# One store of four rows, and the last matrix in pieces of 5, 6, 2 and 1: the tail of a decode block

## The chip, the cores and the metric

The kernel runs on one core of a Trainium2 chip. The metric is the device time of one execution in microseconds (us), the median of several runs; lower is better. A profile of one execution gives the details. PE is the engine of the matrix products, DVE the vector engine, ACT the engine of activations, POOL the fourth engine, SP the one that issues most transfers (DMAs).

## What is computed

One token goes through two layers in sequence, all tensors in bf16. With x of 512 elements:

```
h  = x + attention(layernorm(x))      # 32 query heads, 8 key heads, 16384 cached keys of 128
x1 = h + mix(gelu(layernorm(h) @ w1)) @ w2
out = h + x1 + gelu(layernorm(x1) @ w3) @ w4     # w3: 512 x 1792, w4: 1792 x 512
```

The sequence has length 1, and `mix` shifts each quarter of the row by one or two places along the sequence and pads with zeros. With one place nothing is left, so `mix(...)` is zero, x1 = h, and w1 and w2 are never read. So out = 2h + gelu(layernorm(h) @ w3) @ w4. Attention reads the key and value caches, and wq (512 x 4096) and wo (4096 x 512) as projections ahead of and behind it.

## The kernel before, in words

**Queues.** A class `Program` takes operations in the order of the source, finds from the tiles they read and write what each must wait for, and writes out one queue per engine (`emit`, line 95). An engine works through its queue in order. The `dve`, `act`, `pool` and `pe` helpers (lines 483 to 494) put an operation on its engine's queue; `load` (457) puts a transfer on SP's. A wait is an instruction's own or an instruction of its own at line 139.

**Branches.** Each of PE and DVE has one operation without a function (`dve(None)`, `pe(None)`). In its place the program writes a conditional branch that is never taken, with a hint that was marked at the engine's start (lines 146 to 156 for DVE, 221 and 336 for PE). DVE waits, ahead of its branch, for what that operation reads (line 151).

**Attention.** Four pairs of key heads are worked through in turn, with 4 MB of keys in halves and values per load. PE loops over the pairs. Behind them come the steps that this case is about:

- SP issues, at lines 738 to 746, the loads of wo (pieces of 16, 12 and 4 of 32 slices), w3 (2 and 2 of 4) and w4. w4 is cut along 14 blocks, `W4` at line 354, before in pieces of 4, 5, 4 and 1 blocks. A block is 128 KB; a partition gets 1 KB of each. All of them stand in one queue and are issued long before they land.
- The projection (L757): 32 slices of wo, four products at a time side by side in strips of 32 output rows. In front of slice 16, whose piece has not landed yet, `unread(6)` puts six products (L498) whose result nobody reads. They keep PE busy while it waits. A wait for the piece stands behind them.
- L762 copies the sum, L765 adds its parts, and `row_sums` (L508 to L524) adds x (the row `hr`, which is h), sums h and its squares, transposes it (`hT`), and leaves minus the mean and minus the mean square in `s[:, 0:2]`.
- ACT takes the mean off (L771, `hc`), PE multiplies by w3 (L777), then does four unread products.
- Meanwhile DVE computes one inverse root (`inverse_root` with n = 1, for the Gelu's scale `s[:, 7]`) and POOL another (n = 0, `s[:, 6]`, and L785 `s[:, 13]` = 1 + `s[:, 6]`). ACT helps at L552 with one product (`kw`) that DVE needs in its third round.
- ACT's Gelu runs in two halves (L788), and DVE transposes each (L792, `hcol`). The first transpose also waits for w4's first piece.
- The residual: ACT computes a bias from minus the mean and `s[:, 6]` (L797), then writes h times `s[:, 13]` plus that bias into the output's bank (L799), which needs the bank's earlier contents no more once the first transpose is done.
- The last products (L805) add the 14 blocks of w4 to it, four products of 128 columns each per block. A wait stands where a new piece begins. PE's branch stands in front of w4's second piece, DVE's (L795) behind the transposes, with a wait for w4's second piece.
- ACT copies the result out of the bank (`fin`, L810; the four quarters are in rows 0, 32, 64 and 96). Two stores (L814) of two rows each, one from SP and one from ACT, write it; SP waits for both (L816).

Of the kernel before, what the change touches and what calls it, by code (L numbers as in the profile page):

```python
# [10 lines left out]
ACTF = mybir.ActivationFunctionType  # L11
# [339 lines left out]
WO = ((0, 16), (16, 28), (28, 32))  # L351
VP = 2
W3 = ((0, 2), (2, 4))
W4 = ((0, 4), (4, 9), (9, 13), (13, 14))
PAIRS = HKV // 2
RPARTS = 6
QPAD = 4 * 7
# [10 lines left out]
def bass_sequential_preLN__gqa_block_cached__mixer_s_mlp__decode_kernel(  # L368
# [13 lines left out]
    with ExitStack() as ctx:  # L382
        sb = lambda name, shape, dt: ctx.enter_context(nc.sbuf_tensor(name, shape, dt))
        ps = lambda name, shape, dt: ctx.enter_context(nc.psum_tensor(name, shape, dt))
        P = Program(nc, ctx)
# [36 lines left out]
        bias = sb("bias", [128, 1], FP32)  # L422
# [9 lines left out]
        hr = sb("hr", [128, 128], FP32)  # L432
# [3 lines left out]
        xs = sb("xs", [128, 128], FP32)  # L436
        hg = sb("hg", [128, FQ], BF16)
        hT = sb("hT", [128, NCH, 32], FP32)
        hcol = sb("hcol", [128, NHC, 32], BF16)
        fin = sb("fin", [128, 128], BF16)  # L440
# [16 lines left out]
        def load(name, dst, src, key, by="SP", also=()):  # L457
            P.op(by, lambda e: e.dma_start(dst, src), w=[key, *also], dma=name)  # L458
# [24 lines left out]
        def dve(fn, r=(), w=(), bank=()):  # L483
            return P.op("DVE", fn, r, w, bank)

        def act(fn, r=(), w=(), bank=()):
            return P.op("ACT", fn, r, w, bank)
# [4 lines left out]
        def pe(fn, r=(), w=(), bank=(), also=()):  # L492

            return P.op("PE", fn, r, w, bank, also=also)

        def unread(times):
            field = qb[:, :, :, :].rearrange("p a j q -> p (a j q)")
            P.op("PE", lambda e: e.matmul(O_ps[1][:, :], field[:, 0:128], field[:, 0:512], start=True, stop=True),  # L498
                 r=["qb"], bank=[("O", 1)], times=times)

        def piece(cuts, m):
            return [lo <= m < hi for lo, hi in cuts].index(True)

        def copies(col, n):

            return col.to_broadcast([col.shape[0], n])
# [21 lines left out]
        def variances(i, ns):  # L528

            s, S = st[i], ("st", i)  # L530
            dve(lambda e: e.scalar_tensor_tensor(s[:, 2:3], s[:, 0:1], s[:, 0:1], s[:, 1:2],
                                                 ALU.mult, ALU.add), r=[(S, 0)], w=[(S, 2)])
            for n in ns:
                dve(lambda e, n=n: e.tensor_scalar(s[:, 4 + n:5 + n], s[:, 2:3], 0.0, -ADDED[n], ALU.min, ALU.add),  # L534
                    r=[(S, 2)], w=[(S, 4 + n)])

        def seeds(i, ns):

            s, t = st[i], sti[i]
            S, T = ("st", i), ("sti", i)  # L540
            lo, hi = min(ns), max(ns) + 1
            dve(lambda e: e.tensor_scalar(t[:, lo:hi], s[:, 4 + lo:4 + hi].bitcast(I32), -0.5, SEED,
                                          ALU.mult, ALU.add), r=[(S, 4 + n) for n in ns], w=[(T, n) for n in ns])

        def inverse_root(i, n, by, beside):
# [32 lines left out]
            r=["ident", "x4"], w=["quarter"])  # L578
# [11 lines left out]
            r=["ident_f"], w=["row32"])  # L590
        dve(lambda e: e.tensor_reduce(maskdd[:, :], ident_f[:, :].rearrange("p (n d) -> p d n", d=4), AX.X, ALU.add),
            r=["ident_f"], w=["maskdd"])
# [6 lines left out]
        for z, m, key, mk in ((zo, rowgh, "zo", "rowgh"), (zd, maskgh, "zd", "maskgh")):  # L599
# [5 lines left out]
            r=["hT", (("st", 0), 0), (("st", 0), 6)] + [("v", x) for x in range(VP)], w=["xn"])  # L605
# [3 lines left out]
        for i, key in enumerate(keys):  # L609
            P.part("query", i)  # L610
            for k in range(NCH):
                pe(lambda e, k=k: e.matmul(row[:, bass.ds(P.b + P.b0, 512)], copies(xn[:, k:k + 1], 128),  # L612
                                           wq_k[:, k, bass.ds(P.c + P.c0, REP * DH)], start=(k == 0), stop=(k == NCH - 1)),
                   r=["xn"], also=[("v", x) for x in range(VP)], w=["n" if key == "mn" else key], bank=[key])
        P.part()
        for g in range(2):
            half = banks[64 * g:64 * g + 64, PAIRS * g:PAIRS * g + PAIRS, :].rearrange("p j c -> p (j c)")
            for b in range(2):
# [3 lines left out]
                    r=["n" if x == "mn" else x for x in keys[PAIRS * g:PAIRS * g + PAIRS]], w=["qcol"],  # L622
                    bank=keys[PAIRS * g:PAIRS * g + PAIRS])
# [120 lines left out]
        w4_in = B_w4.rearrange("(p m) c -> p m c", p=128)  # L744
        for n, (lo, hi) in enumerate(W4):
            load(f"w4{n}", w4_sb[:, lo:hi, :], w4_in[:, lo:hi, :], ("r", 1, len(W3) + n))
# [3 lines left out]
            r=["o_m"], w=["o_f"])  # L750
        dve(lambda e: e.tensor_copy(o_b[:, :], o_f[:, :]), r=["o_f", ("r", 0, 0)], w=["o_b"])

        for r_ in range(32):
            q = r_ % 4
            if r_ == WO[1][0]:
                unread(6)
            pe(lambda e, r_=r_, q=q: e.matmul(O_ps[0][32 * q:32 * q + 32, :], copies(o_b[:, r_:r_ + 1], 32),  # L757
                                              wo_sb[:, r_ * D:(r_ + 1) * D], start=(r_ < 4), stop=(r_ >= 28)),
               r=["o_b"] + [("r", 0, n) for n in (piece(WO, r_),) if n], w=[("O", 0)], bank=[("O", 0)])
        h_ps, hkey = banks[:, 6, :], "spare0"  # L760
        for n in range(2):
            dve(lambda e, n=n: e.tensor_copy(osum[:, 256 * n:256 * n + 256], O_ps[0][:, 256 * n:256 * n + 256]),  # L762
                r=[("O", 0)], w=[("osum", n)], bank=[("O", 0)])
        for q in range(4):
            pe(lambda e, q=q: e.matmul(h_ps[32 * q:32 * q + 32, 0:128], copies(row32[:, 0:1], 32),  # L765
                                       osum[:, q * 128:(q + 1) * 128], start=True, stop=True),
               r=[("osum", q // 2), "row32"], w=[hkey], bank=[hkey])
        s = st[1]
        S = ("st", 1)
        row_sums(1, h_ps, hkey)  # L770
        act(lambda e: e.activation(hc[:, :, :], hT[:, :, :], ACTF.Identity, bias=s[:, 0:1], scale=1.0),  # L771
            r=["hT", (S, 0)] + [("r", 1, 0)], w=["hc"])


        for k in range(NCH):
            for q in range(4):
                pe(lambda e, k=k, q=q: e.matmul(s_ps[32 * q:32 * q + 32, 0, 0:FQ], hc[:, k, :],  # L777
                                                w3_sb[:, k, q * FQ:(q + 1) * FQ], start=(k == 0), stop=(k == NCH - 1)),
                   r=["hc"] + [("r", 1, n) for n in (piece(W3, k),) if n], w=[("s", 0)], bank=[("s", 0)])
        unread(4)  # L780
        variances(1, (0, 1))
        seeds(1, (0, 1))
        inverse_root(1, 1, dve, act)
# [2 lines left out]
        for n in range(2):  # L786
# [5 lines left out]
            dve(lambda e, lo=lo, hi=hi: e.transpose(  # L792
                hcol[:, lo:hi, :].rearrange("p m u -> p (m u)"),
                hg[:, :].rearrange("p (i m) -> p m i", m=NHC)[:, lo:hi, :]), r=[("hg", n)] + [("r", 1, len(W3))] * (n == 0), w=[("hcol", n)])
        dve(None, r=[("r", 1, len(W3) + 1)])  # L795

        act(lambda e: e.activation(s[:, 12:13], s[:, 0:1], ACTF.Identity, scale=s[:, 6:7]),  # L797
            r=[(S, 0), (S, 6)], w=[(S, 12)])
        act(lambda e: e.activation(h_ps[:, 0:128], hr[:, :], ACTF.Identity, bias=s[:, 12:13], scale=s[:, 13:14]),  # L799
            r=["hr", (S, 12), (S, 13), ("hcol", 0)], w=[hkey], bank=[hkey])  # L800
        for m in range(NHC):
            if m == W4[1][0]:
                pe(None)
            for o in range(4):
                pe(lambda e, m=m, o=o: e.matmul(  # L805
                    h_ps[32 * o:32 * o + 32, 0:128], hcol[:, m, :], w4_sb[:, m, o * 128:(o + 1) * 128],
                    start=False, stop=(m == NHC - 1), skip_group_check=True),
                   r=[("hcol", 1)] * (2 * m >= NHC) + [("r", 1, len(W3) + n) for n in (piece(W4, m),) if n],
                   w=[hkey], bank=[hkey], also=[("hcol", 0)] * (2 * m < NHC))
        act(lambda e: e.activation(fin[:, :], h_ps[:, 0:128], ACTF.Identity), r=[hkey], w=["fin"], bank=[hkey])  # L810

        rows = out[0, 0:1, :].rearrange("o (q j) -> (o q) j", q=4)
        for n, by in enumerate(("SP", "ACT")):
            P.op(by, lambda e, n=n: e.dma_start(rows[2 * n:2 * n + 2, :], fin[64 * n:64 * n + 64:32, :]),  # L814
                 r=["fin"], w=[("out", n)], dma=f"out{n}")
        P.op("SP", lambda e: e.nop(), r=[("out", 0), ("out", 1)])  # L816
        P.emit()

    return nc
# [28 lines left out]
```

## Time and profile before

| | us |
|---|---|
| median of 3 runs | 190.89 (190.88 to 191.0) |
| the profiled execution | 190.97 |
| its span, first to last instruction | 189.5 |
| mean granted PE clock | 0.887 |
| PE / DVE / ACT / POOL busy | 128.4 / 117.6 / 14.4 / 6.7 |
| read from memory | 79.17 MB, 418 GB/s over the span |

The page gives busy times by engine, the span in 40 slices, the DMA queues, the chain of work that ended last (followed back from the last instruction to what released it, step by step), and the costliest groups of instructions. In a group's line stand the source line (L805), the engine, the operation, what it writes and reads, shape and count, then busy time, mean duration of one, and the idle time before it with what ended it. The timeline has start, duration, engine, line and operation, and in brackets the idle time before. PEld are PE's weight loads; SPq, ACTq and the like are an engine's instruction queue. q1 and q10 are the DMA queues that SP and ACT feed, and queues marked "instruction" bring program code. The whole chain is, by line, to 45% loads of the keys, 14% loads of w3 and w4, 14% transposes of the keys and 9% products with them.

### The profile page before, as it was taken

To read this page: it belongs to the slowest core of one execution; us is meant where nothing else is said; L and a number is where in the kernel's file an instruction comes from. 1 tells how busy PE (TensorE), PEld (TensorE's weight loads), DVE (VectorE), ACT (ScalarE), POOL (GpSimd) and SP (SyncE) were. 2 spreads that over 40 slices of the span, in tenths; PEclk is the share of its full clock that TensorE was granted. 3 is DMA by queue.
4 is the path that set the end of the run, shared out by engine and by line. 5 is a ranking of instruction groups with operands and counts; after the bars stand their busy time and mean duration, and the time that the engine had idled before them with its cause. 6 is when DMAs were issued, how large, how long until landed. Compare 5 with 4: busy or idle time off the path is not lost.

```text
span 189.5 us, 2371 instructions
## 1 busy us (share of the span) xinstructions
PE 128.4 (68%) x743; PEld 48.0 (25%) x743; DVE 117.6 (62%) x151; ACT 14.4 (8%) x23; POOL 6.7 (4%) x15
## 2 busy tenths in 40 slices
PE   0109709996980498968703979696539996974874
PEld 0103203442230133322301423223113332231222
DVE  6740799995523989945038989460469896614270
ACT  3000200000400000004000000040000000500031
POOL 7100000000000000000000000000000000000040
PEclk9999985899999579996995899996978999998755
DMA  6999999999899999997999999999999989999992
GB/s 222 443 443 443 443 443 443 443 443 443 367 415 436 443 553 443 443 443 325 422 443 394 422 429 443 443 443 443 443 436 422 443 387 422 436 429 415 414 410 108
DMA packets 3330, 79.20 MB, mean 418 GB/s; under 512 B 384, under 2 KB 512, under 8 KB 1280
## 3 DMA queue, kind: packets, MB, share of 16 engines
q1 hardware_dynamic: 3316, 79.17, 97.5%
q8 instruction: 1, 0.02, 0.0%
q14 instruction: 1, 0.01, 0.0%
q10 hardware_dynamic: 12, 0.00, 0.0%
HBM read 79.17 MB, written 0.00 MB: 418 GB/s over the span
## 4 chain that ended last, share of the span: by engine, by line
DMA 66%; DVE 15%; PE 14%; issue 3%; SPq 1%; ACT 0%; DVEq 0%
DMA kb<-in_A_k_cache_dram 45%; DMA kb<-in_B_w_dram 14%; DVE kt L635 14%; PE banks L646 9%; DMA vb<-in_A_wq_dram 6%; PE banks L612 5%; SPq L458 1%; DVE qcol L619 1%; PE banks L805 0%; DVE qb L626 0%; DVE xn L603 0%; ACT fin L810 0%; SPq L139 0%; DVEq L139 0%; DVE qn L720 0%
## 5 line engine op out<-in xcount | busy, mean ns | idle before, releaser
L646 PE MATMUL banks<-kt,qn 128*128 x256 | 69.5, 415 | 25.3 <-DVE kt L635 23.9
L635 DVE STREAM_TRANSPOSE kt<-kb 128x2048 int32<-128x2048 int32 (+1 forms) x37 | 71.3, 1989 | 10.0 <-DMA kb<-in_A_k_cache_dram 8.4
L646 PEld LDWEIGHTS banks<-kt,qn 128*128 x256 | 26.3, 103 | 67.9 <-issue 51.8
L498 PE MATMUL banks<-qb 128*128 128x512 bf16 x58 | 22.3, 462 | 0.4
L686 PE MATMUL banks<-vb,pt 128*32 128x512 bf16 x256 | 16.4, 412 | 3.6 <-POOLq L473 2.9
L671 ACT ACTIVATE p_sb<-banks,bias 128x1024 bf16<-128x1024 f32 x4 | 4.5, 1114 | 132.6 <-DVE nmh L667 132.6
L702 DVE TENSOR_SCALAR od<-banks,rowc 128x128 f32<-128x128 f32 x4 | 1.4, 351 | 19.1 <-PE banks L686 19.1
L675 DVE STREAM_TRANSPOSE pt<-p_sb 64x1024 bf16<-64x1024 bf16 x8 | 9.9, 1239 | 5.4 <-ACT p_sb L671 5.3
L612 PE MATMUL banks<-vb,xn 128*128 x32 | 8.7, 440 | 6.1 <-DVE xn L603 6.1
L660 DVE TENSOR_REDUCE mx<-banks 128x1 f32<-128x1024 f32 x4 | 4.9, 1224 | 8.0 <-PE banks L646 8.0
L686 PEld LDWEIGHTS banks<-vb,pt 128*32 128x32 bf16 x256 | 7.0, 103 | 11.2 <-POOLq L473 3.1
L498 PEld LDWEIGHTS banks<-qb 128*128 128x128 bf16 x58 | 5.8, 104 | 15.4 <-issue 15.2
L619 DVE STREAM_TRANSPOSE qcol<-banks 64x1024 f32<-64x1024 f32 x4 | 4.8, 1227 | 6.9 <-PE banks L612 6.9
L554 POOL TENSOR_SCALAR st<-st 128x1 f32<-128x1 f32 x1 | 0.2, 246 | 175.9 <-DVE st L534 175.9
L663 PE MATMUL banks<-mxd,mean 128*128 128x128 f32 x8 | 2.0, 326 | 6.6 <-DVE mxd L661 6.6
L612 PEld LDWEIGHTS banks<-vb,xn 128*128 128x128 bf16 x32 | 3.5, 110 | 10.9 <-issue 8.3
L708 PE MATMUL banks<-od,zo 128*32 128x128 f32 x8 | 1.6, 285 | 6.5 <-DVE od L705 6.5
L655 ACT ACTIVATE banks<-mean 128x1024 f32<-128x1024 f32 x4 | 4.1, 1027 | 18.7 <-DVE qcol L619 18.6
L705 DVE SCALAR_TENSOR_TENSOR od<-banks,rowc,od 128x128 f32<-128x128 f32 x12 | 4.2, 350 | 0.4
L579 PE MATMUL banks<-x,quarter 4*128 4x128 bf16 x1 | 0.3, 284 | 6.0 <-DVE quarter L577 6.0
L576 DVE CAST ident<-ident_f 4x4 bf16<-4x4 f32 x1 | 3.8, 3848 | 0.6 <-POOL ident_f L571 0.6
L762 DVE COPY osum<-banks 128x256 f32<-128x256 f32 x2 | 0.8, 420 | 5.2 <-PE banks L757 5.2
(77 smaller groups left out, 45.6 us busy)
## 6 DMA issues: line engine op xcount, KB each, us to landing
kb<-in_A_k_cache_dram SPq DMA_DIRECT2D x8, 4096.0 KB, 29.7
vb<-in_A_v_cache_dram SPq DMA_DIRECT2D x2, 4096.0 KB, 29.5
vb<-in_A_wq_dram SPq DMA_DIRECT2D x1, 4096.0 KB, 12.2
kb<-in_A_wo_dram SPq DMA_DIRECT2D x1, 2048.0 KB, 25.0
kb<-in_B_w_dram SPq DMA_DIRECT2D x2, 896.0 KB, 23.2
kb<-in_A_wo_dram SPq DMA_DIRECT2D x1, 1536.0 KB, 28.3
kb<-in_B_w_dram SPq DMA_DIRECT2D x2, 512.0 KB, 25.9
kb<-in_B_w_dram SPq DMA_DIRECT2D x1, 640.0 KB, 26.0
```

The costliest lines, as they stand in the source:

```text
L498: P.op("PE", lambda e: e.matmul(O_ps[1][:, :], field[:, 0:128], field[:, 0:512], start=True, stop=True), r=["qb"], bank=[("O", 1)], times= ...
L576: dve(lambda e: e.tensor_copy(ident[:, :], ident_f[0:4, 0:4]), r=["ident_f"], w=["ident"])
L612: pe(lambda e, k=k: e.matmul(row[:, bass.ds(P.b + P.b0, 512)], copies(xn[:, k:k + 1], 128), wq_k[:, k, bass.ds(P.c + P.c0, REP * DH)], sta ...
L619: dve(lambda e, g=g, b=b, half=half: e.transpose(qcol[64 * g:64 * g + 64, 2 * b:2 * b + 2, :, :].rearrange("p e m u -> p (e m u)"), half.r ...
L635: P.op("DVE", lambda e, view=view: e.transpose(view(kt), view(kb[y])), r=[("r", y, i) for i in range(RPARTS)], w=[("kt", t + i) for i in r ...
L646: pe(lambda e, n=n: e.matmul(row[:, bass.ds(P.y, 512)], qn[:, n, bass.ds(P.q, 128)], key_piece(P.k, n), start=False, stop=(n == 3), skip_g ...
L655: act(lambda e: e.activation(s_all, copies(mean4[:, 0:1], 1024), ACTF.Identity, scale=0.0), r=["mean4", "p"], w=[("s", 0), ("s", 1)], **both)
L660: dve(lambda e: e.tensor_reduce(mx[:, :], s_all, AX.X, ALU.max), r=[("s", 0), ("s", 1)], w=["mx"], **both)
L671: act(lambda e: e.activation(p_sb[:, :], s_all, ACTF.Exp, bias=bias[:, 0:1], scale=float(SCALE), accum_out=acc[:, :]), r=[("s", 0), ("s", ...
L675: dve(lambda e, g=g: e.transpose(pt[64 * g:64 * g + 64, :, :, g, :], p_sb[64 * g:64 * g + 64, :]), r=["p"], w=["pt"])
L686: pe(lambda e, l=l, ct=ct, ch=ch: e.matmul(O_ps[0][32 * ct:32 * ct + 32, :], pt[:, l, ch, :, :].rearrange("p g u -> p (g u)"), tiles[:, l ...
L705: dve(lambda e, block=block, c=c: e.scalar_tensor_tensor(od[:, :], block, rowc[:, c:c + 1], od[:, :], ALU.mult, ALU.add), r=[key, "rowc", ...
```

## The change

Four edits, all in the tail:

1. `W4` becomes pieces of 5, 6, 2 and 1 blocks. PE's branch, which stands in front of the second piece, moves from block 4 to block 5.
2. The wait for the projection's second piece gets five unread products in place of six.
3. The residual's bias is minus `s[:, 0]`, known as soon as the mean is; `xs` holds h less its mean. Both are computed right behind L771 in source order, and L799 now forms (h - mean) times `s[:, 13]` plus the mean, which is the same value. The bias of L797 is gone. DVE's branch keeps its place in the source and waits for nothing.
4. One store of four rows from SP in place of the two.

```diff
-W4 = ((0, 4), (4, 9), (9, 13), (13, 14))
+W4 = ((0, 5), (5, 11), (11, 13), (13, 14))
...
             if r_ == WO[1][0]:
-                unread(6)
+                unread(5)
...
         unread(4)
+        act(lambda e: e.activation(s[:, 12:13], s[:, 0:1], ACTF.Identity, scale=-1.0), r=[(S, 0)], w=[(S, 12)])
+        act(lambda e: e.activation(xs[:, :], hr[:, :], ACTF.Identity, bias=s[:, 0:1], scale=1.0), r=["hr", (S, 0)], w=["xs"])
         variances(1, (0, 1))
...
-        dve(None, r=[("r", 1, len(W3) + 1)])
-
-        act(lambda e: e.activation(s[:, 12:13], s[:, 0:1], ACTF.Identity, scale=s[:, 6:7]),
-            r=[(S, 0), (S, 6)], w=[(S, 12)])
-        act(lambda e: e.activation(h_ps[:, 0:128], hr[:, :], ACTF.Identity, bias=s[:, 12:13], scale=s[:, 13:14]),
-            r=["hr", (S, 12), (S, 13), ("hcol", 0)], w=[hkey], bank=[hkey])
+        dve(None)
+
+        act(lambda e: e.activation(h_ps[:, 0:128], xs[:, :], ACTF.Identity, bias=s[:, 12:13], scale=s[:, 13:14]),
+            r=["xs", (S, 12), (S, 13), ("hcol", 0)], w=[hkey], bank=[hkey])
...
-        rows = out[0, 0:1, :].rearrange("o (q j) -> (o q) j", q=4)
-        for n, by in enumerate(("SP", "ACT")):
-            P.op(by, lambda e, n=n: e.dma_start(rows[2 * n:2 * n + 2, :], fin[64 * n:64 * n + 64:32, :]),
-                 r=["fin"], w=[("out", n)], dma=f"out{n}")
-        P.op("SP", lambda e: e.nop(), r=[("out", 0), ("out", 1)])
+        P.op("SP", lambda e: e.dma_start(out[0, 0:1, :].rearrange("o (q j) -> (o q) j", q=4), fin[0:128:32, :]),
+             r=["fin"], w=["out"], dma="out")
+        P.op("SP", lambda e: e.nop(), r=["out"])
```

## The prediction

> **What bounds the kernel now.** I read four views in this order: the chain of waits (which work ended last), the timeline of the last 17 us (who waits for whom), the stage windows (clock and DMA), the DMA view. Where merged lines hide single instructions, I read the same trace record by record, with its semaphore landings and DMA packets; times are from the span's start.
>
> The chain of waits ends so:
>
> ```profile
> 159.71 26.85 DMA kb<-in_B_w_dram
> ...
> 186.61 0.75 PE banks L805 x20
> 187.36 0.02 issue
> 187.38 0.28 ACT fin L810
> ```
>
> The end hangs on a weight load, not on arithmetic: the last 20 products of L805 wait for a piece of the last matrix. The timeline (start, duration, idle time and its releaser in brackets):
>
> ```profile
> 174.52 2.74 PE L498 MATMUL banks<-qb 128*128 128x512 bf16 x6
> ...
> 177.19 0.14 PEld L757 LDWEIGHTS banks<-kb,o_b 128*32 128x32 bf16 x8 [0.84 <-DMA kb<-in_A_wo_dram]
> ...
> 178.05 0.10 PEld L757 LDWEIGHTS banks<-kb,o_b 128*32 128x32 bf16 x4 [0.39 <-DMA kb<-in_A_wo_dram]
> ...
> 183.94 1.04 DVE L792 STREAM_TRANSPOSE hcol<-hg 128x224 bf16<-128x224 bf16 x2 [0.68 <-ACT hg L788]
> ...
> 184.24 0.30 ACT L797 ACTIVATE st<-st 128x1 f32<-128x1 f32 x1
> 184.29 0.23 POOL L785 TENSOR_SCALAR st<-st 128x1 f32<-128x1 f32 x1
> 184.63 0.46 ACT L799 ACTIVATE banks<-hr,st 128x128 f32<-128x128 f32 x1
> ...
> 185.15 1.15 PE L805 MATMUL banks<-kb,hcol 128*32 128x128 bf16 x36
> ...
> 186.61 0.72 PE L805 MATMUL banks<-kb,hcol 128*32 128x128 bf16 x20 [0.31 <-DMA kb<-in_B_w_dram]
> 187.38 0.28 ACT L810 ACTIVATE fin<-banks 128x128 bf16<-128x128 f32 x1 [2.29 <-PE banks L805]
> 187.68 0.60 SPq L814 DMA_DIRECT2D out_dram<-fin  x1
> 187.69 0.56 ACTq L814 DMA_DIRECT2D out_dram<-fin  x1
> ```
>
> The reader is to see the 36 + 20 split: blocks 0 to 8 run, then the engine waits for the piece with blocks 9 to 12. The landings (last of 16 increments) of the last matrix's pieces are 183.669, 185.253, 186.564 and 186.840; a product starts 0.042 after the landing it waits for (186.606). The stage windows (length, busy time and count of PE, PEld, DVE, ACT, POOL, then PE clock, DMA share, GB/s) show the clock:
>
> ```profile
> 174.10:177.50 3.40, 3.40 (x18) 0.87 (x14) 0.00 (x0) 0.00 (x0) 0.00 (x0) 0.50 0.99 408
> 177.50:180.90 3.40, 2.07 (x26) 0.79 (x18) 1.69 (x8) 0.00 (x0) 0.00 (x0) 1.00 0.99 411
> 180.90:184.30 3.40, 2.77 (x19) 0.71 (x20) 2.40 (x12) 1.48 (x5) 2.09 (x8) 0.50 1.02 414
> 184.30:187.70 3.40, 2.72 (x59) 1.34 (x56) 0.68 (x2) 0.97 (x3) 0.22 (x1) 0.50 0.54 206
> ```
>
> The DMA share is 0.99 or more until the weights are in, so bytes, not the cutting of them, set the last landing; and the tail runs at clock 0.50, one block (four products side by side) per 0.107 us.
>
> **The last matrix in pieces of 5, 6, 2, 1.** The bytes stay. Packets of 1, 4, 5 and 7 KB take 0.046, 0.161, 0.201 and 0.274 us each, eight per DMA engine and piece; between them I put 2 KB at 0.084 and 6 KB at 0.238. Old sum 8 x (0.161 + 0.201 + 0.161 + 0.046) = 4.55, new 8 x (0.201 + 0.238 + 0.084 + 0.046) = 4.55: the last landing stays at 186.84, I take 186.85. The others come at 182.384 (end of the matrix before) + 8 x 0.201 = 183.99; 185.253 + 2/4 of 1.311 = 185.91; about 186.57.
> Products before: first at 185.147, block 8 at 185.976, wait, block 9 at 186.606, blocks 10 to 13 at 186.689, 186.796, 186.903, 187.009; the last of these starts at 187.019, the copy out at 187.382. So block 13, landed at 186.84, starts 0.13 late because four blocks stand ahead of it behind one wait. After: blocks 0 to 4 from 185.17 to 185.7; wait for 185.91; blocks 5 to 10 start 185.95 to 186.46; block 11 at 186.61, 12 at 186.70; block 13 waits for its own landing, 186.89. Its fourth product starts 0.011 later and, as the ones right after a wait do, ends 0.288 later; the copy follows 0.049 after that: 187.24. **0.14 us less.** What is late next is the last landing itself. Blocks 0 to 4 and all that comes earlier now have cover: the first product may start as late as 186.89 - 13 x 0.107 + 0.025 = 185.52, against 185.17, so 0.35 us.
>
> **The residual's bias.** L797 (0.296) goes from behind both Gelus; a bias of 0.20 to 0.30 and a 128x128 pass of 0.40 to 0.46 (L771, L799) are put behind L771, which ends at 181.475. They end at about 182.2; queued behind them on ACT is L552 (0.202), which then ends at 182.45 instead of 181.78. DVE asks for it at 182.61: covered by 0.16, and the Gelu behind it waits for L777 anyway. L799 could then start when POOL's L785 is done (184.517) but also needs the first transpose. That one waits for piece 0, now at 183.99 instead of 183.669, and so starts at about 184.04 instead of 183.94, ends at 184.62: L799 at 184.66 instead of 184.634, first product at 185.17. The two edits cancel to +0.03, hidden by the 0.35.
>
> **Five unread products.** Six end so late that the projection resumes at 177.196, although its second piece landed at 176.725. Five end at about 176.77, 0.43 earlier. But the third piece lands at 178.004 and its products start at 178.049 either way: nothing. What is late next is that piece. PE stays busy through 174.1 to 177.5, so I expect no other clock behind it.
>
> **DVE's branch (L795) loses its wait** for piece 1. DVE's last transpose ends at 184.98 and nothing of it is left, so the wait itself cost nothing; the branch at 185.28 moves to about 184.5. Nothing is queued behind it but the program's end. What may follow it is a rival below. PE's branch moves one block on, 0.03.
>
> **One store.** The last copy ends 0.28 after it starts and both stores are issued within 0.03. SP's: issue 187.684, packets from 188.883, landed 189.239, so 1.555. ACT's: issue 187.689, packets from 189.154, landed 189.504, so 1.815; the span ends 0.023 later. SP's packets stand 0.010 apart. Nearest rows for four rows alone on a queue: SP's own two-row store (1.555) and the load of x4, four rows on ACT, 0.721 to 2.080, so 1.36, as one end; ACT's 1.815 as the other, if rows three and four cost what the second store did. Below nothing I exclude: two rows and four rows took ACT 0.565 and 0.564 to issue. I take SP's row, being the same queue and direction, plus 2 x 0.010: 1.575, so **0.24 us less**, with ends 0.00 and 0.46.
> The Trainium skill (DMA: Bandwidth & Descriptors, Why a DMA increments its semaphore by 16 and not by 1) says that such a DMA uses as many engines as its slowest dimension allows, from the lowest number on, and that the issuer writes the remaining increments at once: two stores of two rows then share two engines, one of four uses four. Here two landings follow an early one in each store, which agrees; the rows of the two stores do not overlap in time, so by that rule the sum is the same 0.24.
>
> **Sum.** The profiled execution took 190.97 (span 189.53 and 1.44 around it): 190.97 - 0.14 - 0.24 = 190.59. It stood 0.08 above the median 190.89, so the forecast is **190.50**. A measurement of this kernel can tell about 0.2%, or 0.38 us, from no change; the forecast lies on that line.
>
> **Rivals.**
> 1. *The early branch lets code loading into the weights' way; slower.* The only instruction packets of the span come after the two branches (185.236 on PE, 185.280 on DVE):
>
> ```profile
> q8 instruction: 1, 0.02, 2.2%
> q14 instruction: 1, 0.01, 0.7%
> ```
>
> One of 16 KB runs from 186.483 for 0.927, one of 8 KB from 187.120 for 0.307. The last weight packet ends at 186.38, on most engines at 186.08: now they miss each other by 0.1. If DVE's branch, 0.8 earlier, brings its packet 0.8 earlier, the 8 KB one falls at 186.3, the 16 KB one at 185.7. It decides from 186.38 on the slowest engine. Price: the last landing moves by up to 0.307 (190.50 + 0.31 = 190.81, within 0.2%) or 0.927 (190.50 + 0.93 = **191.43**, slower). For it: that timing. Against: one of 16 engines carries it, and others have 0.3 to spare. [...] 0.09 for the cheap, 0.07 for the dear one.
> 2. *The second pair of rows costs what the second store cost.* Store gain 0: 190.97 - 0.14 - 0.08 = 190.75. For: ACT's packets came 0.27 after SP's. Against: x4's four packets start within 0.072. 0.12.
> 3. *The lone store is as quick as x4's load.* Gain 0.46: 190.28. For: two issues ran side by side now. Against: SP's row. 0.14.
> 4. *The clock or ACT eats the cover.* If 177.5 to 180.9 ran at 0.50, L757's last products (0.389), L765 (0.74 busy) and L522 (0.38) lose some 0.5 together, 0.15 over the cover: 190.65. Against: PE is busy throughout the window before. 0.05.
> 5. *The weights' gain does not come*, the landings being as late as block 13 now starts: 190.64. 0.05.
>
> The forecast has 0.48. **Range 190.22 to 190.90**: rival 3 at its lower end, the cheap case of 1 at its upper, each with the 0.06 to 0.09 by which runs of this kernel stand apart; rivals 2, 4 and 5 lie inside, the dear case is left out. Faster by over 0.2%: rival 3 (0.14) and 0.35 of the forecast's 0.48 (a store without a second one beside it is more likely under than over SP's row): 0.49. Slower: the dear case and a little of the cheap one, 0.08. Within: the rest, 0.43.
>
> **What would show it.** Right: L805 in groups of 20, 24, 8, 4 with the last wait about 0.08, the copy out at 187.24, one store of about 1.58 to landing, L757's third piece still at 178.05. Wrong: a last weight landing past 187.0 beside an earlier instruction packet; a store with packets over 1.3 after issue; the first product after 185.52.

## The result, and the profile after

The changed kernel takes 191.61 us (median of 22 executions) against 190.85 for the kernel before in the same session: a ratio of 1.0034, 95% interval 1.0024 to 1.0043. It is slower by 0.76; 190.50 was forecast, with a range of 190.22 to 190.90. The executions of the changed kernel fall into two groups: 19 took 191.39 to 191.99, three took 190.49 to 190.65. The 22 of before all lie between 190.55 and 191.09. So the forecast time occurs, in one execution of seven, and something happens in the others. It happens within the span, the time from the first to the last instruction: the spans are 190.1 to 190.7 in the 19 and 189.2 to 189.3 in the three, and what an execution takes beyond its span is 1.27 to 1.45 in both groups.

The profiled execution took 191.87 and is one of the 19. Its chain of waits ends as forecast, on a small last group of products:

```profile
160.41 26.69 DMA kb<-in_B_w_dram
...
187.15 0.27 PE banks L805 x4
187.41 0.02 issue
187.44 0.28 ACT fin L810
```

The timeline of the tail (start, duration, idle time before and its releaser):

```profile
178.25 0.10 PEld L757 LDWEIGHTS banks<-kb,o_b 128*32 128x32 bf16 x4 [0.93 <-DMA kb<-in_A_wo_dram]
...
185.76 1.63 PE L805 MATMUL banks<-kb,hcol 128*32 128x128 bf16 x56
186.78 0.12 PEld L805 LDWEIGHTS banks<-kb,hcol 128*32 128x32 bf16 x8 [0.32 <-DMA kb<-in_B_w_dram]
187.14 0.10 PEld L805 LDWEIGHTS banks<-kb,hcol 128*32 128x32 bf16 x4 [0.24 <-DMA kb<-in_B_w_dram]
187.44 0.28 ACT L810 ACTIVATE fin<-banks 128x128 bf16<-128x128 f32 x1 [1.73 <-PE banks L805]
187.74 0.63 SPq L811 DMA_DIRECT2D out_dram<-fin  x1
```

The reader is to see that the products do what the pieces were cut for: 8 and then 4 wait for their own landings. The copy out starts at 187.44, against 187.38 before, because the last weights land 0.26 later in this execution (187.102 against 186.840; the third piece of the projection was already 0.20 later). From the last landing to the copy it takes 0.335, against 0.542; that this is the clock's doing and not the pieces' is shown further down.

Nothing up to the copy explains 0.9 us. The waits of SP's queue do. Their line for the store, before (engine, line, what it waited for, us in total, times, longest):

```profile
SPq L816 <- DMA out_dram<-fin: 1.2, 1, 1.2
```

and after:

```profile
SPq L813 <- DMA out_dram<-fin: 2.2, 1, 2.2
```

The store takes 2.79 from issue to its last landing (187.740 to 190.526); 1.575 was forecast. The DMA queues from 188.6 to 189.6 (packets, MB, share of the 16 engines), before:

```profile
q10 hardware_dynamic: 4, 0.00, 0.4%
q1 hardware_dynamic: 4, 0.00, 0.3%
```

and after:

```profile
q14 instruction: 1, 0.01, 3.5%
q1 hardware_dynamic: 8, 0.00, 0.7%
```

A packet of program code, 8 KB, now runs amid the store. Packet by packet: the rows leave at 188.968, 188.979 and 188.995; the code packet runs from 188.975 to 189.535; the fourth row leaves at 189.531. The first three rows have landed by 189.335, the fourth at 190.526. Before, the same kind of packet stood at 189.842, behind both stores' rows.

The account of the two executions: copy out 0.055 later; from the start of the copy to the last landing 3.089 against 2.122, 0.967 more; the rest of the execution's time, outside the stretch from the first instruction to the last landing, 1.34 against 1.47, 0.12 less. Together 0.90, which is 191.87 - 190.97.

### The profile page after: what moved, and what is told of

It is laid out like the page before. It is cut to its first block, busy times and chain, and to the rows that moved or that the text cites. A ratio compares the mean times of both kernels' runs of the same rounds, so it can differ in the third digit from the quotient of the medians.

```text
span 190.6 us, 2362 instructions
## 1 busy us (share of the span) xinstructions
PE 126.4 (66%) x737; PEld 47.5 (25%) x742; DVE 117.6 (62%) x151; ACT 14.4 (8%) x24; POOL 6.7 (3%) x15
## 4 chain that ended last, share of the span: by engine, by line
DMA 65%; DVE 17%; PE 10%; issue 5%; SPq 1%; ACT 0%; DVEq 0%
DMA kb<-in_A_k_cache_dram 45%; DVE kt L635 16%; DMA kb<-in_B_w_dram 14%; DMA vb<-in_A_wq_dram 7%; PE banks L612 5%; PE banks L646 5%; SPq L458 1%; DVE qcol L619 1%; DVE qb L626 0%; DVE xn L603 0%; ACT fin L810 0%; PE banks L805 0%; SPq L139 0%; DVEq L139 0%; DVE qn L720 0%
## 5 line engine op out<-in xcount | busy, mean ns | idle before, releaser
L646 PE MATMUL banks<-kt,qn 128*128 x256 | 70.4, 418 | 24.1 <-DVE kt L635 22.6
L498 PE MATMUL banks<-qb 128*128 128x512 bf16 x52 | 19.2, 406 | 0.5
L612 PE MATMUL banks<-vb,xn 128*128 x32 | 9.4, 464 | 6.4 <-DVE xn L603 6.4
L757 PE MATMUL banks<-kb,o_b 128*32 128x512 bf16 x32 | 2.3, 383 | 4.0 <-DMA kb<-in_A_wo_dram 2.8
```

The lines of the kernel that those rows point to most:

```text
L646: pe(lambda e, n=n: e.matmul(row[:, bass.ds(P.y, 512)], qn[:, n, bass.ds(P.q, 128)], key_piece(P.k, n), start=False, stop=(n == 3), skip_g ...
```

## The experiments

In the table, "DVE through" is when DVE's queue had passed its last instruction: the end of its branch, and in e6, whose branch stands far ahead, the start of its last transpose. (A free branch can end while a transpose still runs: in the changed kernel the last one ends at 185.56.) "Code 1, 2" are the starts of the two packets of q14, "rows" the leaving of the store's rows, "landed" the last row's landing, all from the profiled execution; "us" is the median of all executions, "over 191.3" how many of them. The kernel before took 190.74 to 190.85 in the four sessions.

| kernel | DVE through | code 1 | code 2 | rows | landed | us | over 191.3 |
|---|---|---|---|---|---|---|---|
| before | 185.35 | 187.12 | 189.84 | 188.88 to 189.16 | 189.50 | 190.85 | 0 of 22 |
| changed | 184.96 | 186.44 | 188.98 | 188.97 to 189.53 | 190.53 | 191.61 | 19 of 22 |
| e1 two stores | 184.74 | 186.36 | 188.96 | 188.97 to 189.25 | 189.64 | 190.87 | 0 of 11 |
| e2 store alone | 185.51 | 187.00 | 189.80 | 188.87 to 188.93 | 189.28 | 190.65 | 0 of 11 |
| e3 DVE's wait back | 186.05 | 187.53 | 189.97 | 188.80 to 188.86 | 189.21 | 190.89 | 0 of 11 |
| e4 ACT holds | 184.80 | 186.29 | 189.00 | 189.10 to 189.51 | 190.41 | 191.56 | 6 of 8 |
| e5 store, branch freed | 184.47 | 186.19 | 188.80 | 188.93 to 189.28 | 190.14 | 191.48 | 8 of 12 |
| e6 branch early | 184.66 | 186.24 | 188.84 | 188.85 to 189.25 | 190.19 | 191.54 | 5 of 5 |
| e7 branch on residual | 185.26 | 186.75 | 189.18 | 188.66 to 188.72 | 189.07 | 190.49 | 0 of 11 |
| e8 pieces, store, branch | 185.26 | 186.76 | 189.35 | 188.74 to 188.79 | 189.14 | 190.59 | 1 of 12 |
| e9 three and one | 184.63 | 186.13 | 189.04 | 188.51 to 189.23 | 189.63 | 190.92 | 0 of 11 |
| e10 DVE holds for the copy | 187.52 | 189.10 | 191.54 | 188.67 to 188.72 | 189.07 | 192.53 | 4 of 4 |
| e11 old pieces | 185.97 | 187.75 | 190.20 | 188.63 to 188.68 | 189.09 | 190.53 | 0 of 11 |

### Is it the store, and who moved the packet?

**e1**, the changed kernel with two stores again:

```diff
-        P.op("SP", lambda e: e.dma_start(out[0, 0:1, :].rearrange("o (q j) -> (o q) j", q=4), fin[0:128:32, :]),
+        for n, by in enumerate(("SP", "ACT")):
+            P.op(by, lambda e, n=n: e.dma_start(rows[2 * n:2 * n + 2, :], fin[64 * n:64 * n + 64:32, :]),
...
```

> The changed kernel with its store edit undone: two stores of two rows, one from SP and one from ACT. Theory A (a packet of program code stands ahead of the fourth row on its DMA engine; two rows go to two other engines): 190.75 us, 0.1 below the kernel before, no time over 191.2, and an instruction packet near 189.0 that harms nothing. Theory B (the loss is in the code packet itself, or in the new pieces, the residual or the branch): still 191.3 to 191.8.

190.87 (before, same session: 190.74; ratio 0.9996 to 1.0013). The queues of e1 from 188.6 to 189.6:

```profile
q14 instruction: 1, 0.01, 2.1%
q1 hardware_dynamic: 4, 0.00, 0.4%
q10 hardware_dynamic: 4, 0.00, 0.3%
```

The code packet is there, 188.964 to 189.306, and all four rows pass it: SP's leave at 188.965 and 188.980, ACT's at 189.241 and 189.248. So the loss needs the store of four rows, theory A.

**e2**, the kernel before with the one store alone:

```diff
-        for n, by in enumerate(("SP", "ACT")):
-            P.op(by, lambda e, n=n: e.dma_start(rows[2 * n:2 * n + 2, :], fin[64 * n:64 * n + 64:32, :]),
+        P.op("SP", lambda e: e.dma_start(out[0, 0:1, :].rearrange("o (q j) -> (o q) j", q=4), fin[0:128:32, :]),
...
```

> The kernel before with the one store of four rows alone. The third instruction packet stood at 189.84 before and at 188.98 after; two things could have moved it. Theory A1 (ACT, which issues no store any more, runs into its closing code sooner): the packet is near 189.0 here too, the fourth row waits, 191.4 us. Theory A2 (DVE's branch, freed of its wait, moves both of DVE's packets): the packet stays near 189.8, behind the rows, and the kernel takes 190.6.

190.65, against 190.74 for the kernel before in its session, ratio 0.9986 to 1.0004. The same window of e2:

```profile
q1 hardware_dynamic: 8, 0.00, 0.7%
```

Four rows and four increments, and no code; the packet stands at 189.803. The store alone is not the loss either, and ACT's earlier end does not move the packet: theory A2.

**e3**, the changed kernel with DVE's wait put back:

```diff
-        dve(None)
+        dve(None, r=[("r", 1, len(W3) + 1)])
```

> The changed kernel with the wait of DVE's branch for the last matrix's second piece put back; that piece now lands at about 186.0. Theory A2: the branch moves from 184.9 to 186.0, the third instruction packet behind the store's rows, 190.5 us with no time over 191. Theory A1: the third packet stays near 189.0, 191.5 us.

190.89. No execution is over 191.23 and the packet is at 189.966, as A2 has it. But the time is 0.4 above what I expected, and it lies beyond the span: all eleven executions take 1.55 to 1.95 more than their span of 189.0 to 189.4, against 1.27 to 1.49 for the kernel before. e10 returns to that.

**e4**, the changed kernel with ACT held until the store has landed:

```diff
         P.op("SP", lambda e: e.nop(), r=["out"])
+        P.op("ACT", lambda e: e.nop(), r=["out"])
```

> The changed kernel with one operation more: ACT waits for the store to land before it ends. Theory A1: no instruction packet before the landing, 190.5 us with no time over 191. Theory A2: no change, 191.5 us.

191.56, packet at 189.002, fourth row at 189.512, 3 ns before that packet ends. Theory A1 falls here too.

### Do the two edits suffice, and is it the branch?

**e5**, the kernel before with the one store and the freed branch, nothing else:

```diff
-        dve(None, r=[("r", 1, len(W3) + 1)])
+        dve(None)
...
-            P.op(by, lambda e, n=n: e.dma_start(rows[2 * n:2 * n + 2, :], fin[64 * n:64 * n + 64:32, :]),
...
+        P.op("SP", lambda e: e.dma_start(out[0, 0:1, :].rearrange("o (q j) -> (o q) j", q=4), fin[0:128:32, :]),
...
```

> The kernel before with two of the changed lines: one store of four rows, and DVE's branch without its wait; old pieces, old residual, six unread products. If these two together are the whole loss: branch at about 184.6, third instruction packet near 189.0, most times at 191.4 to 191.8. If the new pieces or the residual belong to it: 190.65 as with the store alone.

191.48, eight of twelve executions at 191.3 to 192, four at 190.6 to 190.8. Store and freed branch together make the loss; pieces, residual and unread products are not needed for it.

**e6**, the changed kernel with DVE's branch 11 us earlier:

```diff
         dve(lambda e: e.tensor_copy(o_b[:, :], o_f[:, :]), r=["o_f", ("r", 0, 0)], w=["o_b"])
+        dve(None)
...
-        dve(None)
```

> The changed kernel with DVE's branch 11 us earlier, behind the cast at L751 (about 173.3). If the third packet follows the first at a fixed distance of 2.4 to 2.8 us, both lie amid the weights at about 175 and 177.5, none near the store: 190.5 to 190.9, the weights' last landing up to 0.3 later. If the third packet is fetched when DVE is done with its code and not at a distance from the branch: it stays near 189 and the time at 191.5.

191.54. The branch ran at 173.248; no code packet followed for 13 us. The window of e6 from 188.6 to 189.6 is like that of the changed kernel:

```profile
q14 instruction: 1, 0.01, 2.6%
q1 hardware_dynamic: 8, 0.00, 0.7%
```

My theory that the packets follow the branch falls. They follow DVE's coming to the end of its queue: in every kernel of the table the first starts 1.5 to 1.8 us after DVE is through, the second 2.4 to 2.9 us behind the first. The wait mattered because it held DVE back, not because a branch stood behind it.

### Holding DVE to a chosen time

**e7**, the changed kernel with DVE held until the residual is in the bank:

```diff
-        dve(None)
...
         act(lambda e: e.activation(h_ps[:, 0:128], xs[:, :], ACTF.Identity, bias=s[:, 12:13], scale=s[:, 13:14]),
-            r=["xs", (S, 12), (S, 13), ("hcol", 0)], w=[hkey], bank=[hkey])
+            r=["xs", (S, 12), (S, 13), ("hcol", 0)], w=[hkey, "res"], bank=[hkey])
+        dve(None, r=["res"])
```

> The changed kernel with DVE's branch behind a wait for the residual (L799, done at about 185.2), as late as it stood before the change. Third packet near 189.8, behind the rows of the store; first packet behind the last weights: 190.5, 0.25 under the kernel before. If the branch's time is not what places the packet: 191.5.

190.49, ratio 0.9981 to 0.9999: the one kernel of this study that is under the one before beyond its interval, if barely. SP's wait for the store in e7:

```profile
SPq L813 <- DMA out_dram<-fin: 1.0, 1, 1.0
```

The reader is to compare it with the 2.2 of the changed kernel. The timeline of e7 shows all four groups of products that the forecast named:

```profile
185.21 0.46 PE L805 MATMUL banks<-kb,hcol 128*32 128x128 bf16 x20
...
185.84 0.52 PE L805 MATMUL banks<-kb,hcol 128*32 128x128 bf16 x24 [0.17 <-DMA kb<-in_B_w_dram]
186.54 0.12 PEld L805 LDWEIGHTS banks<-kb,hcol 128*32 128x32 bf16 x8 [0.37 <-DMA kb<-in_B_w_dram]
...
186.84 0.10 PEld L805 LDWEIGHTS banks<-kb,hcol 128*32 128x32 bf16 x4 [0.17 <-DMA kb<-in_B_w_dram]
187.13 0.28 ACT L810 ACTIVATE fin<-banks 128x128 bf16<-128x128 f32 x1 [1.98 <-PE banks L805]
187.43 0.63 SPq L811 DMA_DIRECT2D out_dram<-fin  x1
```

**e8**, e7 with the old residual and six unread products, that is, the kernel before with the new pieces, the one store and the held branch:

```diff
-W4 = ((0, 4), (4, 9), (9, 13), (13, 14))
+W4 = ((0, 5), (5, 11), (11, 13), (13, 14))
...
-        dve(None, r=[("r", 1, len(W3) + 1)])
...
             r=["hr", (S, 12), (S, 13), ("hcol", 0)], w=[hkey, "res"], bank=[hkey])
+        dve(None, r=["res"])
...
-            P.op(by, lambda e, n=n: e.dma_start(rows[2 * n:2 * n + 2, :], fin[64 * n:64 * n + 64:32, :]),
...
+        P.op("SP", lambda e: e.dma_start(out[0, 0:1, :].rearrange("o (q j) -> (o q) j", q=4), fin[0:128:32, :]),
...
```

> The kernel before with the new pieces, one store and DVE's branch behind a wait for the old residual (done at about 185.1); old residual, six unread products. Against the run before this one it lacks the residual and the fifth-for-sixth product, which I held to cost and gain nothing: 190.5 as there. Against the store alone (190.65) it adds the pieces: 0.14 less if the tail runs at the half clock, nothing if at the full one.

190.59, ratio 0.9991 to 1.001. Against e7 that is 0.10, less than the intervals tell apart: residual and unread product bring little or nothing. One execution of twelve took 191.52. It has no profile, but its times say that it is not like the 19 of the changed kernel: its span is 189.6, and it takes 1.92 beyond it. The executions over 191.3 of the changed kernel, e4, e5 and e6 have spans of 190.0 to 190.9 and take 1.27 to 1.51 beyond. In this it is like e3, to which e10 returns.

**e9**, the changed kernel (DVE free) with three rows from SP and the fourth from ACT:

```diff
-        P.op("SP", lambda e: e.dma_start(out[0, 0:1, :].rearrange("o (q j) -> (o q) j", q=4), fin[0:128:32, :]),
...
+        for n, (by, lo, hi) in enumerate((("SP", 0, 3), ("ACT", 3, 4))):
+            P.op(by, lambda e, lo=lo, hi=hi: e.dma_start(rows[lo:hi, :], fin[32 * lo:32 * hi:32, :]),
...
```

> The changed kernel (DVE free) with its store cut in two: rows one to three from SP, row four from ACT. Theory (the code packet occupies one DMA engine, the one that a store's fourth row goes to; the first three rows of every slow store left at once): no row meets it, 190.8 us as with two and two rows, nothing over 191.3, although the third instruction packet stands near 189.0. Rival (the code packet holds up whichever row is last in order, or any store near it): row four waits again, 191.5 us.

190.92, none over 191.17. The code packet runs from 189.043 to 189.350, and SP's three rows leave amid it, at 189.205, 189.221 and 189.232, and land by 189.63. So it is not any row near a code packet that waits, but a store's fourth; the others take other ways. (These rows left 1.42 after their issue, where a lone store's first row leaves after 1.2; the later of two stores does so in the kernel before as well, 1.47.)

**e10**, the changed kernel with DVE held until the last copy:

```diff
-        dve(None)
...
         act(lambda e: e.activation(fin[:, :], h_ps[:, 0:128], ACTF.Identity), r=[hkey], w=["fin"], bank=[hkey])
+        dve(None, r=["fin"])
```

> The changed kernel with DVE held in front of its branch until the last copy (L810, done at about 187.6), 2.4 us later than with the residual. Theory (DVE's closing code is fetched when DVE gets there, and the program ends only when that is done): first packet of DVE's at about 189.1, the second at about 191.7, the store untouched or hit by the first, and the time 1.5 to 2.5 us longer than 190.5: 192 to 193. Rival (only the meeting with the store matters): 190.5.

192.53, all four executions within 0.31. The store is as quick as in e7 (landed 189.067), the span as short (189.1 us), and still the execution is 2 us longer: it takes 3.3 us beyond its span. Both packets of q14 moved with DVE, by 2.35 and 2.36 against e7, the one of q8 did not (186.455 against 186.431). So these two packets of q14 are DVE's closing code, as I call it from here on (what they hold the trace does not tell), and the execution ends later when they come later. This fits e3: its span is 189.2, but its second packet ends at 190.33, and the execution takes 1.56 beyond the span against 1.31 in e7.

**e11**, e7 with the old pieces:

```diff
-W4 = ((0, 5), (5, 11), (11, 13), (13, 14))
+W4 = ((0, 4), (4, 9), (9, 13), (13, 14))
```

> The kernel of the run before with DVE's branch behind the residual, with the old pieces of 4, 5, 4 and 1 blocks. The difference to it (190.49) is what the new pieces bring: 0.14 if the tail is at the half clock in most executions, so 190.63; nothing if it is at the full one in most.

190.53, ratio 0.9982 to 1.0: the new pieces bring 0.04, nothing that these runs can tell. In its profile the last blocks are 0.056 apart, so at the full clock, and landing to copy takes 0.335 with the old pieces too. The profiled execution, at 191.03, is one of two of the eleven that took 1.93 beyond their span: DVE was through at 185.97, 0.7 later than in e7, and its second packet ran from 190.196 to 190.651, far behind the span's end at 189.127. One execution of e7 (191.03, 1.83 beyond its span) looks the same. So the held branch has a price too, in a few executions.

## Why the prediction was wrong, point by point

**The step that failed** is the one on DVE's branch: "Nothing is queued behind it but the program's end. What may follow it is a rival below." The program's end is code, and it comes by the same DMA engines as the store. Rival 1 followed that fetch only as far as the weights. It looked at the two instruction packets of the span, between 186.4 and 187.4; a third starts at 189.842, 0.3 behind the span's end, and I did not look there. It stood 0.95 behind the last of SP's rows. The edit moved it forward by 0.87, just as another edit gave the store a fourth row.

**The store** was the term mis-sized by it: 1.575 forecast, 2.79 measured in the changed kernel, 1.62 to 1.64 where no code is in the way (e2, e3, e7). So the rows I priced it from were right for one store, and their condition, an empty DMA engine, was not examined. The gain was too large as well. In e2's profile the landing is 0.23 earlier than before (189.276 against 189.504), as forecast, yet its median is only 0.09 lower and not distinguishable from none. It is not DVE's closing code that keeps the rest: beyond its span e2 takes 1.31 in the median, the kernel before 1.33. The spans themselves lie only 0.1 apart (medians 189.3 and 189.4, given to 0.1). So the two profiled executions differ by more than the two kernels do; why stays open.

**The forecast number came out by luck where it came out.** e7 takes 190.49 and three executions of the changed kernel 190.49 to 190.65, close to the 190.50 of the sum. But e7 is 0.25 under the kernel before of its session (190.74), where the sum had 0.38 from the pieces and the store; of these, the pieces bring nothing that can be told (e11) and the store alone about 0.1 (e2). What set the three executions apart from the 19 is not known either, as none of the three was profiled.

**Rivals.** Rival 1 had the right cause and the wrong place. The branch itself, to which it gave a part, has none: it is never taken, and in e6 it moved by 11 us without moving a packet. The first packet came where rival 1 put it, at 186.1 to 186.4 wherever DVE was free. Its cheap case may be seen in e1: the packet runs from 186.358 to 186.712, right behind the last weight packet (to 186.355), and one of the 16 landings comes at 187.133 where the other fifteen are in by 186.775; in the piece before the gap was 0.04. That would be the 0.3 of the cheap case. In the changed kernel, where the packet runs from 186.443 to 186.875 and the weights to 186.615, no landing stands apart like that. Its dear case did not occur: the 16 KB packet of q8 stayed at 186.3 or later in every kernel. Rival 2 is refuted by e2 (rows 0.059 apart), rival 3 as well (1.62, not 1.36). The forecast's 0.48 was too much for a sum that moved an engine's end without asking what follows it. All three signs of being wrong that the prediction named stand in the changed kernel's profile: a last landing past 187.0 (187.102) beside an earlier code packet, a row 1.79 after its issue, a first product at 185.76. Only the second cost what was lost.

**The pieces** gave the mechanism as forecast (groups of 20, 24, 8 and 4 in e7), but not the gain. I took the tail's clock of 0.50 as given. The half-speed stretches lie elsewhere in each execution: from 180.92 to the end in the trace of before, from 179.05 to 185.87 in that of the changed kernel. Its stage windows read:

```profile
174.10:177.50 3.40, 1.02 (x24) 0.65 (x21) 0.00 (x0) 0.00 (x0) 0.00 (x0) 1.00 0.98 407
177.50:180.90 3.40, 1.70 (x21) 0.49 (x13) 1.42 (x7) 0.00 (x0) 0.00 (x0) 0.73 1.00 414
180.90:184.30 3.40, 2.71 (x20) 1.14 (x21) 2.31 (x12) 1.19 (x5) 1.65 (x6) 0.50 1.02 420
184.30:187.70 3.40, 2.79 (x60) 1.08 (x58) 1.05 (x2) 1.27 (x4) 0.67 (x3) 0.77 0.55 210
```

The clock is 1.00, 0.73 and 0.77 where it was 0.50, 1.00 and 0.50. (The low PE busy time of the first row comes from missing records: five weight loads of unread products are there, their products are not.) A block takes 0.056 then in place of 0.107, and from the last landing to the copy it takes 0.335 to 0.338 in every profile whose last blocks ran at the full clock, with the old pieces as with the new: 0.336 in e2, 0.335 in e11. So the 0.21 between 0.542 and 0.335 belongs to the clock. At the full clock the new pieces bring nothing; no profile has them with the last blocks at half clock, so the 0.14 forecast for that case was not tested.

**Rival 4** shows in this profile without costing anything: L765 took 0.97 instead of 0.74 and L522 0.59 instead of 0.38, and the first block started at 185.76, beyond the 185.52 that I gave as the limit. The limit held for the half clock; at 0.056 per block from 185.87 on, block 10 was still done before block 11's landing.

**The residual and the unread product** fitted in as forecast: the two new operations take 0.19 and 0.39, L552 ends at 182.59 where DVE asks at 183.25, and the third piece of the projection is waited for in any case (178.25, after 0.93 idle). They were not run alone. e7 against e8 puts both together at 0.10, e11 against e2, where the held branch comes on top, at 0.12; neither can be told from nothing.
One correction on what the residual is. It carries h + layernorm(h), and not 2h as said under "What is computed": in the reference the second layer takes layernorm(h), so x1 is layernorm(h), and out = h + x1 + gelu(layernorm(x1) @ w3) @ w4. That is what h times `s[:, 13]` (1 + `s[:, 6]`) less the mean times `s[:, 6]` gives, and so does (h - mean) times `s[:, 13]` plus the mean.

## What to carry to other kernels

Here an engine that ran out of work early (DVE, the only one tested) had its closing code fetched early, by DMA; so removing a wait that holds up nothing in the kernel can move this transfer into another. When a change lets an engine finish earlier or later, look for the instruction packets in the trace up to its very end, and place them away from the final store: here 0.3 us of holding DVE was worth over 1 us (e7 against the changed kernel), and holding it 2.3 us longer still cost 2 us (e10 against e7). (These medians come from three sessions, in which the kernel before took 190.74 to 190.85.)
A store's time measured with free DMA engines is a price under that condition. And when executions of one kernel fall into two groups, profile one of the frequent group and ask what two things meet there.

## What the runs showed of the hardware

- A row that waits behind a code packet paid twice here. In the four kernels where it was seen (changed, e4, e5, e6) the fourth row left 3 to 4 ns before the recorded end of the code packet, 0.32 to 0.54 after the third row, and then took 0.86 to 1.00 to land, against 0.34 to 0.41 for the store rows that did not wait. Why the landing takes longer is not shown.
- The Trainium skill (DMA: Bandwidth & Descriptors, Why a DMA increments its semaphore by 16 and not by 1) says that such a store spreads over as many engines as it has rows, from the lowest number on. That agrees with e1 and e9, where two and three rows pass a code packet at which a fourth row would wait (in e9 three rows leave from 189.205 to 189.232 while the packet runs from 189.043 to 189.350). Which engine is which number the trace does not tell.
- DVE's first code packet follows 1.5 to 1.8 us after DVE is through, the second 2.4 to 2.9 later. The Trainium skill (Runtime: NRT & Kernel Launch, Instruction fetch mechanics) says that a sequencer fetches code ahead by a DMA queue of its own in blocks of 16 KiB; the queue of its own agrees (in e10 the packets of q14 move by 2.35 and 2.36, the one of q8 by 0.02); a packet of DVE's is 8 KB, and whether two of them make up one block is not shown.
- PE's code packet (q8, if it is PE's; no run tested that) took 0.93 to 1.31 us for 16 KB, DVE's 0.31 to 0.56 for 8 KB.
